# Pair 0 of an attention kernel: its split, its first scores and the last bias transfers in another place

## The chip, the cores and the metric

The kernel runs on one core of a Trainium2 chip. The metric is the device time of one execution in microseconds: 673.65 us is the median of three runs before the change (672.23 to 676.15). Times inside the trace count from the start of the span.

## The reference, cut to what matters

Attention with a bias that a small network computes from relative positions, then an MLP with ELU. There are 4 batches, 8 heads, 576 positions and 64 dimensions; the hidden size of the bias network is 32.

```python
scores = scale * np.matmul(q, k.transpose(0, 1, 3, 2))
x = (psi_rel / psi_i)[..., None]          # psi_rel = log1p|i-j|, psi_i = log1p(max(i,1))
h = np.maximum(x @ w1 + b1, 0.0)          # hidden 32
bias = h @ w2                             # one value per head
attn = softmax(scores + bias)             # over the last axis
x = (attn @ v) as (2304, 512)
out = elu(x @ w_in) @ w_out               # w_in 512 x 2048, w_out 2048 x 512
```

All arithmetic is float32 or better; the MLP's weights arrive as 64-bit floats and are decoded on the chip.

## The kernel before

The order of the instructions is written out by hand. Each engine takes its own in that order, and a waiting instruction holds up all that stand behind it on its engine. The program has three stages.

**The bias phase** (`bias_phase`, L130 to L257) makes the bias of all heads, in 36 sets of four position blocks each. A set takes four relus (L199 on ScalarE for g = 0, L201 on VectorE for the other three), eight matrix products into a pair of PSUM banks (`mix`, L209), and a scaled copy out of them (`place`, L222, ScalarE). Two sets make one buffer `bo`, and one transfer of 576 KB carries it into the tile `bias` (L231, on SyncE's queue); the sets of the small tile `biast` go in four transfers a buffer (L237). The relus run two sets ahead of the products. There are twelve relu buffers and four `bo` buffers. Sets 20 to 35 make the bias of the row chunks 2 and 3.

**Attention** (`attention`, L531 to L698) goes over 16 pairs of heads. For a pair, `load_pair` (five transfers, L98 to L102) fetches K and Q, and `split_high` and `split_low` (L118, L122) write each as a sum of a high and a low part; three products of those parts make the scores (`scores`, L299). Five chunks of rows are worked on, u = 0 to 4, u = 4 being the 64 last rows of both heads in one. For each, the order strings (L540) hold the steps: S the scores, X one head's step, which adds the bias and finds the row's extreme (L319, VectorE) and then takes the exponential (L330, ScalarE), T the transposes (L387), P the copies out of them (L406) into `pta` (chunks 0, 1, 4) or `ptb` (2, 3), V the product with the values, C the copy of the result, M and Q the 64 last columns. A token's letter `a` is the pair itself, `y` the pair before it, so a pair's later steps lie in the next pair's lines.

Before the change pair 0 follows the same five lines as the others: S0 X00 X01, S1 X10 X11, S4 T0 P00A X40, S2 T1 P01A P10A X20 X21, S3 T4 and so on. Its own split stands behind the last set (L255, L256; both halves on VectorE, while for later pairs the low half runs on GpSimd). Next come, on SyncE, the load of the first block of the MLP's weights (`decode`, L268), pair 0's values (L127) and, in line 2, pair 2's K and Q.

From pair 1 on, each pair also decodes a block of weights: `dm` from `raw` on VectorE (L277, in line 0, ahead of that pair's X00), `da` from `raw` on GpSimd (L273), the sign (L281), the shift (L283), the sum (L286).

Memory is handed out as a stack of pools. The pools of the bias phase (before the change `bc`, `bw` with the relus, `bop` with the `bo` buffers) are closed at its end, and the pools of the attention (`pta`, `ssp`, `ptb`, `xp`, `dq` with `da` and `dm`) take over the same bytes in order. PSUM has eight banks: four for score pairs (`sp`, also used by `mix`), three for transposes (`wp`), one for V (`vp`).

**The MLP** (L700 on) is a long run of matrix products.

Of the kernel before, what the change touches and what calls it, by code (L numbers as in the profile page):

```python
# [10 lines left out]
F32 = mybir.dt.float32  # L11
# [5 lines left out]
PSUM = bass.MemoryType.PSUM  # L17
# [7 lines left out]
def kernel(  # L25
# [11 lines left out]
    nc = tc.nc  # L37
# [21 lines left out]
    dpool = ctx.enter_context(tc.tile_pool(name="dpool", bufs=1, space=DRAM))  # L59
    ps1 = ExitStack()  # L60
    sp = ps1.enter_context(tc.tile_pool(name="sp", bufs=2, space=PSUM))
    wp = ps1.enter_context(tc.tile_pool(name="wp", bufs=3, space=PSUM))
    vp = ps1.enter_context(tc.tile_pool(name="vp", bufs=1, space=PSUM))
    ident = const.tile([P, P], F32, name="ident")

    bias = const.tile([P, NCH // 2, H, 2, S], F32, name="bias")
# [10 lines left out]
    qd = [[big.tile([P, P], F32R, name=f"qd{m}{i}") for i in range(2)] for m in range(2)]  # L77
    sts = [big.tile([P, S], F32, name=f"st{i}") for i in range(2)]

    def w_bank(name):  # L80
        return wp.tile([P, 512], F32, tag="w", name=name)

    def v_bank(name):
        return vp.tile([P, 512], F32, tag="v", name=name)

    def pair_bank(name):
        return sp.tile([P, 2, 512], F32, tag="ps", name=name)
# [41 lines left out]

    def bias_phase():  # L130
        with (
            tc.tile_pool(name="bc", bufs=1) as bc,
            tc.tile_pool(name="bw", bufs=12) as bw,
            tc.tile_pool(name="bop", bufs=4) as bop,
        ):


            NS = S // 16
            T = bc.tile([P, TW], F32, name="T")
            cs = bc.tile([P, 2 + 4 * H], F32, name="cs")  # L140
            psi = bw.tile([P, 4, NG], F32, tag="rel", name="psi")
            inr = bc.tile([P, 4, NS], F32, name="inr")
            SC = bc.tile([P, NS, 4], F32, name="SC")
            inv = bc.tile([P, NS // 4, 4], F32, name="inv")
            RIM = S - 64 + 48 + 3
            cut = RIM - P - 48


            def load_T(u0, u1, eng):
                for i in range(4):  # L150
                    row, off = (0, TOFF - RIM - 4 * i) if 4 * i <= TOFF - RIM else (i, TOFF + i - RIM - 4 * i)
                    hid = slice(32 * row, 32 * row + 32)
                    eng.dma_start(out=T[32 * i:32 * i + 32, u0:u1], in_=rtab[hid, u0 + off:u1 + off])

            tiny = bc.tile([P, 1], F32, name="tiny")
            for t in qd[0] + qd[1]:
                nc.gpsimd.memset(t.bitcast(F32), 0.0)
            nc.vector.memset(tiny, 0.0)
            for i in range(4):
                nc.scalar.dma_start(out=psi[32 * i:32 * i + 32], in_=cst[:, 0:NG].rearrange("(s c) n -> c s n", s=4))  # L160
            nc.sync.dma_start(out=cs, in_=cst[:, NG:NG + 2 + 4 * H])
            load_T(cut, RIM + S, nc.sync)
            load_T(0, cut, nc.sync)

            nc.scalar.activation(tiny, tiny, AF.Relu)
            for i in range(4):
                nc.scalar.dma_start(
                    out=inr[8 * i:8 * i + 8],
                    in_=cst[32 * i:32 * i + 32, NG + 2 + 4 * H:].rearrange("(s h) n -> h s n", s=4),
                )  # L170

            load_pair(0)
            load_pair(1)
            w1c, b1c = cs[:, 0:1], cs[:, 1:2]
            W2 = cs[:, 2:]

            for i in range(4):
                q = slice(32 * i, 32 * i + 32)
                sc = SC[q].rearrange("p k s -> p s k"), psi[q].rearrange("p s (k i) -> p s k i", i=4)[:, :, :, i]
                if i % 2:  # L180
                    nc.scalar.activation(*sc, AF.Copy, scale=b1c[q])
                else:
                    nc.vector.tensor_scalar(*sc, b1c[q], None, op0=ALU.mult)
            nc.vector.tensor_scalar(T[:, cut:RIM + S], T[:, cut:RIM + S], w1c, None, op0=ALU.mult)

            sets = [(2 * (c + o) + y, s) for c in (0, 2) for s in range(4) for y in range(2) for o in range(2)]
            sets[16:16] = [(2 * NCH, s) for s in range(4)]
            rels, pss = {}, {}

            def relu(s):  # L190
                B, x = sets[s]
                rels[s] = []
                for g in range(4):
                    u = RIM - 64 * B - 16 * g - x
                    src = T[:, u:u + S]
                    b = SC[:, 4 * B + g, x:x + 1]
                    rel = bw.tile([P, S], F32, tag="rel", name="rel")
                    if g == 0:
                        nc.scalar.activation(rel, src, AF.Relu, bias=b)  # L199
                    else:  # L200
                        nc.vector.tensor_scalar(rel, src, b, 0.0, op0=ALU.add, op1=ALU.max)  # L201
                    rels[s].append(rel)

            def mix(s):
                rel = rels.pop(s)
                ps = pss[s] = pair_bank("bps")
                for f in range(2):
                    for g in range(4):
                        nc.tensor.matmul(  # L209
                            ps[32 * g:32 * g + 32, f, 0:HS],  # L210
                            lhsT=W2,
                            rhs=rel[g][:, f * HS:(f + 1) * HS],
                            start=True,
                            stop=True,
                        )

            def place(s):
                if s % 2 == 0:
                    pss["bo"] = bop.tile([P, 2, S], F32, tag="bo", name="bo")
                bo = pss["bo"]  # L220
                B, x = sets[s]
                nc.scalar.activation(  # L222
                    bo[:, s % 2].rearrange("p (f x) -> p f x", f=2), pss.pop(s)[:, :, 0:HS],
                    AF.Copy, scale=inv[:, B, x:x + 1],
                )
                if s % 2 == 0:
                    return
                B, x = sets[s - 1]
                if B < 2 * NCH:
                    q0 = 64 * (B % 2) + x  # L230
                    nc.sync.dma_start(out=bias[q0:q0 + 61:4, B // 4], in_=bo)  # L231
                    return
                for e in range(2):
                    src = bo.rearrange("(i e) s x -> i e s x", e=2)[:, e]
                    for o in range(2):
                        q0 = TAIL * e + x + o
                        nc.sync.dma_start(out=biast[q0:q0 + 61:4], in_=src[:, o])  # L237

            AHEAD = 2
            for s in range(AHEAD):  # L240
                relu(s)
            for g in range(4):
                q = slice(32 * g, 32 * g + 32)
                nc.vector.tensor_copy(
                    inv[q].rearrange("p b s -> p s b"), inr[0:32].rearrange("p s (b g) -> p s b g", g=4)[:, :, :, g],
                )
            nc.vector.tensor_scalar(T[:, :cut], T[:, :cut], w1c, None, op0=ALU.mult)
            for s in range(NS):
                mix(s)
                if s > 0:  # L250
                    place(s - 1)
                if s + AHEAD < NS:
                    relu(s + AHEAD)
            place(NS - 1)
            split_high(0)  # L255
            split_low(0, nc.vector)  # L256
            decode(dp, 0, "load")  # L257

# [29 lines left out]
            nc.sync.dma_start(out=wf[f], in_=a.bitcast(F32))  # L288


    def scores(n, u):
        (kh, kl), (qh, ql) = nat[n]
        heads = range(2 if u < NCH else 1)
        st["ps", n, u] = [pair_bank("ps") for e in heads]
        for f in range(2):
            for t, (q, k) in enumerate(((0, kh), (0, kl), (1, kh))):
                for e, ps in zip(heads, st["ps", n, u]):
# [233 lines left out]
    def attention():  # L531

        pool = lambda name, bufs=1: ph1.enter_context(tc.tile_pool(name=name, bufs=bufs))
        pta, st["ssp"], ptb = pool("pta"), pool("ssp", 3), pool("ptb")
        xp = ph1.enter_context(tc.tile_pool(name="xp", bufs=2))
        st["dq"] = pool("dq")

# [8 lines left out]
        )  # L546
        LATE = (
# [45 lines left out]
        def step(N, line):  # L593
            for tok in line.split():
# [15 lines left out]
                if k == "S":  # L610
                    if i[0] == 0:
# [1 line left out]
                            pl.tile([P, NU, q], F32, tag=t, name=t)  # L613
                            for pl, t, q in ((pta, "pta", QA), (ptb, "ptb", QB))
                        ]
                    scores(n, i[0])
                elif k == "X":
                    expo(n, *i)
                elif k == "T":
# [26 lines left out]
        def aside(n, i):  # L646
            if i == 1:
                weights(n - 2, "store")
            if i == 0:
                load_v(n)  # L650
            if i == 2:
                if n + 2 < NP:
                    load_pair(n + 2)
            if n == 0 and i == 2:
                split_high(1)
                split_low(1)
            if n > 0 and n % HP == 0:
# [18 lines left out]
                high_w(1)  # L676

        for n in range(NP):
            for i, line in enumerate(STEPS if n < NP - 4 else LATE):
                flush()  # L680
                step(n, line)
                aside(n, i)
# [366 lines left out]
```

## Time and profile before

| | |
|---|---|
| median of three runs | 673.65 us (672.23 to 676.15) |
| the profiled execution | 670.85 us |
| its span | 668.7 us |
| TensorE busy | 651.7 us, 97% of the span |
| VectorE, ScalarE, GpSimd busy | 481.9, 450.1, 134.3 us |
| bias phase, products | 7.68 to 55.71 us |

A busy share is an average over all stages. Idle time of an engine costs only where something that ends the run waits for it, so the rows below are taken from single stretches. `PEld` is TensorE's weight load, `SPq` SyncE's queue, `ACTq`, `POOLq` and `DVEq` the sequencers of ScalarE, GpSimd and VectorE. A row such as `[0.62 <-issue]` says how long the engine had been idle and what ended that.

### The profile page before, as it was taken

Reading aid. Unit: us, or ns where it says so; the run is one execution under the profiler, and the core shown is the slowest. Engines: PE = TensorE matmul, PEld = TensorE weight load, DVE = VectorE, ACT = ScalarE, POOL = GpSimd, SP = SyncE. Lnnn points to the kernel's source line nnn. Section 1 sums busy time; section 2 is a strip of 40 time slices with the busy share of each in tenths; the row PEclk is TensorE's granted clock in tenths of the full one; section 3 lists DMA queues with packets and bytes.
Section 4 is the critical chain, followed back from the end, with each engine's and each line's share of the span. In section 5 each row is a group of like instructions: output and inputs, shape, how many; then the busy total and the mean of one; then the engine's idle time right before and its main releaser. Section 6 shows DMA issues by size and latency. Waiting matters only on the chain.

```text
span 668.7 us, 13838 instructions
## 1 busy us (share of the span) xinstructions
PE 651.7 (97%) x5246; PEld 522.8 (78%) x5246; DVE 481.9 (72%) x999; ACT 450.1 (67%) x981; POOL 134.3 (20%) x172
## 2 busy tenths in 40 slices
PE   5998999999999999999999999999999999999997
PEld 3545677777667677688898988989989898998986
DVE  6997888888888899887878998645465654444443
ACT  6996999999999899756655676544444544443343
POOL 0000655565566656410000000000000000000000
PEclk9997999999999999999999999999999999999999
DMA  6999557797677866664799669986854565454102
GB/s 161 217 228 243 160 176 196 227 268 225 197 234 222 261 194 173 214 208 124 238 326 348 250 265 341 351 302 223 264 196 196 203 255 238 196 197 174 64 1 94
DMA packets 49938, 144.63 MB, mean 216 GB/s; under 512 B 13376, under 2 KB 26448, under 8 KB 42192
## 3 DMA queue, kind: packets, MB, share of 16 engines
q1 hardware_dynamic: 47840, 141.08, 65.4%
q10 hardware_dynamic: 2032, 2.67, 1.2%
q8 instruction: 41, 0.67, 0.4%
q14 instruction: 25, 0.20, 0.1%
HBM read 92.14 MB, written 40.97 MB: 199 GB/s over the span
## 4 chain that ended last, share of the span: by engine, by line
PE 88%; DMA 4%; DVE 3%; ACT 2%; issue 1%; SPq 1%; POOL 0%; DVEq 0%; ACTq 0%; POOLq 0%
PE acc L793 29%; PE h L842 25%; PE wv L429 11%; PE ps L299 10%; PE bps L209 7%; PE wt L387 5%; DMA kk<-in_k_dram 1%; DMA raw<-in_wd_dram 1%; DVE ss L319 1%; PE wm L361 1%; DMA T<-in_rtab_dram 1%; DVE bias L518 1%; SPq L473 1%; DMA wa<-wf 1%; PE wt L395 0%
## 5 line engine op out<-in xcount | busy, mean ns | idle before, releaser
L793 PE MATMUL acc<-wB,gh 128*128 128x512 f32 x528 | 171.3, 392 | 0.0
L842 PE MATMUL h<-bias 128*128 128x384 f32 x552 | 111.6, 339 | 1.3 <-DVE e L821 1.3
L319 DVE CUSTOM_DVE_ANT_0 ss<-ps,bias 128x576 f32<-128x576 f32 x128 | 91.7, 753 | 24.4 <-PE ps L299 10.0
L793 PEld LDWEIGHTS acc<-wB,gh 128*128 128x128 f32 x528 | 98.1, 188 | 14.3
L842 PEld LDWEIGHTS h<-bias 128*128 128x128 f32 x552 | 99.7, 188 | 9.5 <-DVE e L821 2.4
L330 ACT ACTIVATE ss<-ss,nm 128x576 f32<-128x576 f32 x128 | 99.4, 780 | 10.0 <-DVE nm L319 9.6
L793 PE MATMUL acc<-wB,gl 128*128 128x512 f32 x264 | 103.8, 393 | 0.0
L822 ACT CAST gh<-e 128x384 fp32r<-128x384 f32 x96 | 49.4, 514 | 42.3 <-DVE e L821 41.4
L827 ACT ACTIVATE e<-c 128x384 f32<-128x384 f32 x66 | 34.7, 525 | 53.4 <-DVE c L873 53.4
L816 DVE TENSOR_TENSOR gl<-e,gh 128x384 fp32r<-128x384 f32 x96 | 53.1, 553 | 19.2 <-ACT gh L822 16.8
L827 ACT ACTIVATE e<-h 128x384 f32<-128x384 f32 x28 | 13.8, 491 | 68.3 <-PE h L842 68.3
L821 DVE SCALAR_TENSOR_TENSOR e<-e,c 128x384 f32<-128x384 f32 x66 | 36.7, 556 | 30.6 <-ACT e L828 30.5
L842 PE MATMUL h<-bias,wA 128*128 128x384 f32 x276 | 56.3, 338 | 0.0
L793 PEld LDWEIGHTS acc<-wB,gl 128*128 128x128 f32 x264 | 49.5, 187 | 7.8
L209 PE MATMUL bps<-rel,cs 128*32 128x288 f32 x576 | 48.0, 424 | 7.7 <-ACT rel L199 7.7
L429 PE MATMUL wv<-pta,vv 128*64 128x320 f32 (+1 forms) x320 | 53.6, 447 | 0.0
L842 PEld LDWEIGHTS h<-bias,wA 128*128 128x128 f32 x276 | 50.2, 188 | 3.8
L828 ACT ACTIVATE e<-e 128x384 f32<-128x384 f32 x96 | 50.5, 526 | 3.0
L299 PE MATMUL ps<-kh,qh 64*128 64x288 f32 x256 | 48.4, 345 | 3.1 <-DVE nm L319 2.6
L873 DVE TENSOR_TENSOR c<-h,u 128x384 f32<-128x384 f32 x66 | 36.7, 555 | 20.1 <-PE h L842 20.1
L387 PEld LDWEIGHTS wt<-ident,ss 64*128 64x128 f32 x1024 | 41.9, 140 | 9.6 <-issue 6.9
L333 POOL TENSOR_SCALAR md<-ss 128x128 f32<-128x128 f32 x64 | 22.2, 347 | 133.1 <-ACT ss L330 131.8
(127 smaller groups left out, 1195.7 us busy)
## 6 DMA issues: line engine op xcount, KB each, us to landing
wB<-wB SPq DMA_DIRECT2D x22, 1024.0 KB, 4.8
raw<-in_wd_dram SPq DMA_DIRECT2D x16, 1024.0 KB, 6.1
bias<-wA SPq DMA_DIRECT2D x9, 1792.0 KB, 9.0
wA<-wA SPq DMA_DIRECT2D x8, 1792.0 KB, 11.8
wa<-wf SPq DMA_DIRECT2D x20, 512.0 KB, 5.2
bias<-bo SPq DMA_DIRECT2D x16, 576.0 KB, 7.7
wA<-bias SPq DMA_DIRECT2D x5, 1792.0 KB, 14.4
wf<-da SPq DMA_DIRECT2D x16, 512.0 KB, 6.8
```

Source lines behind the costliest of these rows:

```text
L209: nc.tensor.matmul(ps[32 * g:32 * g + 32, f, 0:HS], lhsT=W2, rhs=rel[g][:, f * HS:(f + 1) * HS], start=True, stop=True,)
L299: nc.tensor.matmul(ps[:, f, 0:HS], lhsT=(qh, ql)[q][r, u * P:(u + 1) * P] if u < NCH else qd[n % 2][q], rhs=k[r, f * HS:(f + 1) * HS], sta ...
L319: nc.vector.tensor_tensor_reduce(out=s.rearrange("p (f x) -> p f x", f=2), in0=st["ps", n, u][e][:, :, 0:HS], in1=bap.rearrange("p (f x) - ...
L330: nc.scalar.activation(s, s, AF.Exp, bias=nm, scale=-1.0, accum_out=st["sm", b][:, hp, col:col + 1])
L387: nc.tensor.transpose(banks[r][:, x * TAIL:(x + 1) * TAIL], ss[q, c:c + P], ident[q, q])
L429: nc.tensor.matmul(st["pv", n, half][e * D:(e + 1) * D, 0:N], lhsT=l, rhs=r, start=start, stop=stop)
L793: nc.tensor.matmul(acc[j, t], lhsT=x[:, t * P:(t + 1) * P], rhs=w, start=(count[j, t] == 1), stop=(count[j, t] == 6 * NQ),)
L816: nc.vector.tensor_sub(gl, t, gh.bitcast(F32))
L822: nc.scalar.copy(g[i, e][0][:, h * HB:(h + 1) * HB], t)
L827: nc.scalar.activation(t, src, AF.Relu, scale=-1.0)
L828: nc.scalar.activation(t, t, AF.Exp, scale=-1.0)
L842: nc.tensor.matmul(ps, lhsT=a[f][c], rhs=x[y][c], start=(start and k == 0), stop=(stop and k == len(todo) - 1), skip_group_check=not start,)
```

## The change

Six things change.

1. PSUM: in the bias phase the four banks of `wp` and `vp` form a pool `ip` of two double banks; `open_banks` closes it behind line 1 of pair 0 and opens `wp` and `vp` there.
2. Pair 0's split moves from behind the last set to behind the relus that are issued with set 18.
3. Pair 0's S0 is issued ahead of set 31, into `ip`; its S1 goes into `ip` too.
4. Pair 0 gets an order of its own, FIRST: S4 stands ahead of X00, and each of the later scores earlier than in STEPS. Pair 1's split stands behind line 1.
5. Sets 33 and 35 send their buffer head by head, in eight transfers of 72 KB each. Heads 0 and 1 go at once; then come the weights, V of pair 0, heads 2 and 3 of both buffers, pair 2's K and Q, heads 4 to 7 of both.
6. The relu buffers become three pools of four, `psi` moves into a `bo` buffer, `bc` goes to the end of the stack, and `ssp` is opened ahead of `pta`.

```diff
+    ps0 = ExitStack()
+    ip = ps0.enter_context(tc.tile_pool(name="ip", bufs=2, space=PSUM))
+    def open_banks():
+        ps0.close()
+        for k, n in (("w", 3), ("v", 1)):
+            banks[k] = ps1.enter_context(tc.tile_pool(name=k + "p", bufs=n, space=PSUM))
...
-            tc.tile_pool(name="bw", bufs=12) as bw,
-            tc.tile_pool(name="bop", bufs=4) as bop,
+            tc.tile_pool(name="bw0", bufs=4) as bw0,
+            tc.tile_pool(name="bw1", bufs=4) as bw1,
+            tc.tile_pool(name="bw2", bufs=4) as bw2,
+            tc.tile_pool(name="bop", bufs=4) as bop,
             tc.tile_pool(name="bc", bufs=1) as bc,
...
-                    nc.sync.dma_start(out=bias[q0:q0 + 61:4, B // 4], in_=bo)
+                    dst = bias[q0:q0 + 61:4, B // 4]
+                    if s < NS - 4:
+                        nc.sync.dma_start(out=dst, in_=bo)
+                        return
+                    src = bo.rearrange("(k h) s x -> k h s x", h=H)
+                    parts = [(dst[:, h], src[:, h]) for h in range(H)]
+                    later.extend(parts[2:])
+                    send(parts[:2])
...
             for s in range(NS):
+                if s == NS - 5:
+                    scores(0, 0, first_bank)
                 mix(s)
...
+                if s == NS // 2:
+                    split_high(0)
+                    split_low(0, nc.vector)
             place(NS - 1)
-            split_high(0)
-            split_low(0, nc.vector)
             decode(dp, 0, "load")
+            load_v(0)
+            send(later[0:2] + later[6:8])
+            load_pair(2)
+            send(later[2:6] + later[8:])
...
-        pta, st["ssp"], ptb = pool("pta"), pool("ssp", 3), pool("ptb")
+        st["ssp"], pta, ptb = pool("ssp", 3), pool("pta"), pool("ptb")
+        FIRST = (
+            "aS0 aS4 aX00 aX01 aX40",
+            "aS1 aX10 aX11",
+            "aS2 aT0 aP00A",
+            "aT1 aP01A aP10A aX20 aX21",
+            "aS3 aT4 aP11V aP40A aP41A aX30 aX31",
+        )
-            if i == 0:
+            if i == 0 and n > 0:
                 load_v(n)
             if i == 2:
-                if n + 2 < NP:
+                if 0 < n < NP - 2:
                     load_pair(n + 2)
-            if n == 0 and i == 2:
+            if n == 0 and i == 1:
+                open_banks()
                 split_high(1)
                 split_low(1)
```

## Rows read from the trace of the kernel before

**Rows 1.** Stretches: length, busy time of each engine, granted clock, DMA share, GB/s.
```profile
80.00:90.00 10.00, 10.00 (x123) 6.84 (x122) 8.20 (x21) 9.45 (x26) 5.94 (x9) 1.00 0.41 103
58.50:65.30 6.80, 5.69 (x39) 4.77 (x41) 3.81 (x14) 3.62 (x9) 0.60 (x2) 0.50 1.01 245
64.50:68.50 4.00, 3.40 (x55) 3.05 (x52) 3.23 (x11) 3.57 (x8) 2.68 (x3) 0.90 1.02 320
```
**Rows 2.** Groups by line, 20 to 50 us: busy, mean ns, idle before.
```profile
L201 DVE TENSOR_SCALAR rel<-T,SC 128x576 f32<-128x576 f32 x71 | 30.6, 509 | 0.0
...
L209 PEld LDWEIGHTS bps<-rel,cs 128*32 128x32 f32 x370 | 14.3, 108 | 15.8 <-DVE rel L201 6.7 <-ACT bo L222 3.4
```
**Rows 3.** VectorE in order of time, end of the bias phase: start, length.
```profile
54.52 0.39 DVE L118 CAST qd<-qq 64x64 fp32r<-64x64 f32 x2
...
56.93 0.45 DVE L122 TENSOR_TENSOR qd<-qq,qd 64x64 fp32r<-64x64 f32 x2
58.00 0.76 DVE L319 CUSTOM_DVE_ANT_0 ss<-ps,bias 128x576 f32<-128x576 f32 x1 [0.62 <-issue]
```
**Rows 4.** The chain of waits, 55 to 78 us: start, length, what.
```profile
55.74 0.75 ACT bo L222
...
59.50 1.58 PE ps L299 x10
...
73.81 0.98 PE ps L299 x9
...
76.35 0.79 PE ps L299 x6
```
**Rows 5.** ScalarE in order of time, pair 0.
```profile
58.80 0.78 ACT L330 ACTIVATE ss<-ss,nm 128x576 f32<-128x576 f32 x1 [2.32 <-DVE nm L319]
...
59.58 0.76 ACT L330 ACTIVATE ss<-ss,nm 128x576 f32<-128x576 f32 x1
...
66.19 1.06 ACT L406 COPY pta<-wt 128x512 f32<-128x512 f32 x2
...
70.59 0.76 ACT L330 ACTIVATE ss<-ss,nm 128x576 f32<-128x576 f32 x1
```
**Rows 6.** VectorE in order of time, pairs 0 and 1.
```profile
65.98 0.76 DVE L319 CUSTOM_DVE_ANT_0 ss<-ps,bias 128x576 f32<-128x576 f32 x1 [0.25 <-PE ps L299]
...
69.25 0.75 DVE L319 CUSTOM_DVE_ANT_0 ss<-ps,bias 128x576 f32<-128x576 f32 x1
...
69.92 0.69 DVE L277 TENSOR_SCALAR dm<-raw 128x1024 int32<-128x1024 uint32 x1
71.34 0.76 DVE L319 CUSTOM_DVE_ANT_0 ss<-ps,bias 128x576 f32<-128x576 f32 x1 [0.72 <-PE ps L372]
...
74.84 0.76 DVE L319 CUSTOM_DVE_ANT_0 ss<-ps,bias 128x576 f32<-128x576 f32 x1
```
**Rows 7.** SyncE's issues in order of time.
```profile
57.09 0.58 SPq L268 DMA_DIRECT2D raw<-in_wd_dram  x1
57.73 1.82 SPq L127 DMA_DIRECT2D vv<-in_v_dram  x1
59.65 0.52 SPq L98 DMA_DIRECT2D kk<-in_k_dram  x1
...
61.54 1.32 SPq L102 DMA_DIRECT2D qq<-in_q_dram  x2
```
**Rows 8.** Issues in ns and landings in us: of `biast`, of `kk`, of `bias`.
```profile
L237 SPq DMA_DIRECT2D biast<-bo x8: 533/561/595, 32.1 to 38.1; - x8
...
DMA to landing us min/median/max: 2.3/2.5/2.7
...
DMA to landing us min/median/max: 7.2/7.7/8.5
```
**Rows 9.** Semaphore rows ahead of the first write of `da` and of `ptb`.
```profile
L273 POOLq EVENT_SEMAPHORE  x4: 17/43/43, 71.5 to 71.7; - x4
...
L406 ACTq EVENT_SEMAPHORE  x2: 38/38/38, 72.1 to 72.2; - x2
```

More of the change, by code (lines that the diff above doesn't have):

```diff
@@ L61 @@
     sp = ps1.enter_context(tc.tile_pool(name="sp", bufs=2, space=PSUM))
-    wp = ps1.enter_context(tc.tile_pool(name="wp", bufs=3, space=PSUM))
-    vp = ps1.enter_context(tc.tile_pool(name="vp", bufs=1, space=PSUM))
+    ps0 = ExitStack()
+    ip = ps0.enter_context(tc.tile_pool(name="ip", bufs=2, space=PSUM))
+    banks = {}
     ident = const.tile([P, P], F32, name="ident")
@@ L78, with first_bank @@
     sts = [big.tile([P, S], F32, name=f"st{i}") for i in range(2)]
+    def open_banks():
+        ps0.close()
+        for k, n in (("w", 3), ("v", 1)):
+            banks[k] = ps1.enter_context(tc.tile_pool(name=k + "p", bufs=n, space=PSUM))
     def w_bank(name):
-        return wp.tile([P, 512], F32, tag="w", name=name)
+        return banks["w"].tile([P, 512], F32, tag="w", name=name)
     def v_bank(name):
-        return vp.tile([P, 512], F32, tag="v", name=name)
+        return banks["v"].tile([P, 512], F32, tag="v", name=name)
+    def first_bank(name):
+        return ip.tile([P, 2, 512], F32, tag="ps", name=name)
     def pair_bank(name):
@@ L140, in bias_phase @@
             cs = bc.tile([P, 2 + 4 * H], F32, name="cs")
-            psi = bw.tile([P, 4, NG], F32, tag="rel", name="psi")
+            psi = bop.tile([P, 2, S], F32, tag="bo", name="psi")[:, 0].rearrange("p (s n) -> p s n", s=4)
             inr = bc.tile([P, 4, NS], F32, name="inr")
@@ L196, in relu @@
                     b = SC[:, 4 * B + g, x:x + 1]
-                    rel = bw.tile([P, S], F32, tag="rel", name="rel")
+                    rel = (bw0, bw1, bw2)[s % 3].tile([P, S], F32, tag="rel", name="rel")
                     if g == 0:
@@ L237, in place, with send @@
                         nc.sync.dma_start(out=biast[q0:q0 + 61:4], in_=src[:, o])
+            later = []
+            def send(parts):
+                for dst, src in parts:
+                    nc.sync.dma_start(out=dst, in_=src)
             AHEAD = 2
@@ L288, in decode, with scores @@
             nc.sync.dma_start(out=wf[f], in_=a.bitcast(F32))
-    def scores(n, u):
+    def scores(n, u, bank=pair_bank):
         (kh, kl), (qh, ql) = nat[n]
         heads = range(2 if u < NCH else 1)
-        st["ps", n, u] = [pair_bank("ps") for e in heads]
+        st["ps", n, u] = [bank("ps") for e in heads]
         for f in range(2):
@@ L615, in step @@
                         ]
-                    scores(n, i[0])
+                    if ("ps", n, i[0]) not in st:
+                        scores(n, i[0], first_bank if (n, i[0]) == (0, 1) else pair_bank)
                 elif k == "X":
@@ L678, in attention @@
         for n in range(NP):
-            for i, line in enumerate(STEPS if n < NP - 4 else LATE):
+            for i, line in enumerate(FIRST if n == 0 else STEPS if n < NP - 4 else LATE):
                 flush()
```

## The prediction

> **What bounds the kernel now.** I began with the table by stretches. From about 70 us on TensorE is full (10.00 of 10 us in [rows 1], first row) and VectorE is not (8.20), and the page keeps it so to the end; a microsecond that pair 0 or the bias phase gives or takes is therefore given or taken by the whole span. Then the groups by line in the bias phase: VectorE's three relus of a set stand with no idle time (71 in 30.6 us, 0.0 idle, [rows 2]), while TensorE's weight loads idle 15.8 us of the same 30, mostly for those relus. 30.6/71 is 0.43 us a relu, 1.29 us a set: VectorE sets the pace of the bias phase. Third, VectorE's own rows at the end of it [rows 3]: the last relu is followed by pair 0's split, 54.52 to 57.38, and then VectorE waits for TensorE, 0.62 us before the first score-plus-bias step (X00). The chain of waits [rows 4] runs from ScalarE's last copy over pair 0's scores (1.58 us for what takes 0.98 at 73.81) into a run of TensorE alone, and the granted clock is 0.50 from 58.5 to 65.3 us ([rows 1], second row). Last come ScalarE [rows 5], VectorE in pair 1 [rows 6] and SyncE's issues [rows 7].
>
> I write S, X, T, V as in the order strings, and X00(1) for pair 1.
>
> **Part 1, the split amid the sets.** The same eight instructions, 57.38 - 54.52 = 2.86 us [rows 3], move into a queue that has no gap [rows 2]. Nothing on VectorE hides them, so every later relu, the last matrix products and ScalarE's last scaled copy come 2.86 us later: that copy, 55.74 to 56.49 [rows 4], ends at 59.35. In the old place about 1.9 us of them lay beside TensorE's and ScalarE's last set. TensorE starves some 2 us at set 21. Below: no further cost, the value I take, since it waits half its time anyway [rows 2]. Above: the clock falls to the lower level as at 58.5 [rows 1] and two sets take 0.6 us longer, +1.3 us (an estimate: a set's 1.29 us less the idle half, doubled).
>
> **Part 2, scores ahead.** Pair 0's S0 now sits ahead of set 31 on TensorE, in banks of its own: about 0.9 us beside waits for relus, cost 0 (0 to 0.5). VectorE goes from its last relu (57.4) straight into X00 at 57.4 and X01 at 58.1 instead of 58.00 and 58.69 [rows 3]. TensorE leaves set 35 at about 58.4; S4 takes 1.0 (its tail is 0.79 at the higher clock, [rows 4]) and S1 0.9 more, so X40 starts at 59.5, X10 at 60.3, X11 ends at 61.8, pair 1's three casts take 1.1, and X20 follows at 62.9. S3 needs the banks of X20 and X21; X31 starts at 66.1, against 69.25 [rows 6]: 3.1 us earlier. ScalarE is behind that: the first exp waits for the scaled copy, 59.3 (58.80 before). To the last exp of the pair lie eight pitches of 59.58 - 58.80 = 0.78, three copies of 0.53 and two smaller ones (0.4 each, an estimate from the 0.53), 8.6 in all [rows 5]: 67.9 against 70.59, 2.7 earlier. So this part, with part 1 inside it, would give **-2.7 us**, if nothing after it waited. The first two pieces of the last set's bias are issued at 59.4 and 60.0 and land by 62.5, so X20 hardly waits (before it waited 0.25 for TensorE, [rows 6]).
>
> **Part 3, the transfers by head.** Here is what is late next. Two issues of 576 KB become 16 of 72 KB, four of them ahead of the weight load. After the last scaled copy SyncE now has 21 issues in one run. Their pace: pieces of the small bias tile cost 0.56 us each and 0.04 between [rows 8], so 0.6; weight load to V load 0.64, V load to the next 1.92, pair 2's five issues 59.65 to 62.90, 3.25 [rows 7]. The last of the 21 starts at 59.4 + 2 x 0.6 + 0.64 + 1.92 + 4 x 0.6 + 3.25 + 7 x 0.6 = 73.0, and lands 2.5 later by the K rows [rows 8]: 75.5. With the 533 ns minimum for every piece, 0.6 for the V load and 2.3 of landing it is 73.1; with half the issue time for an eighth of the rows, 70.1; a second slow issue makes 77.4. I take **74.5**, near the sum by the nearest rows.
>
> Who waits for that? The late pieces read the `bo` buffers, whose memory the attention's pools take over. The trace shows how such a takeover is guarded: the first write of `ptb` carries two extra semaphore rows and the first write of `da` four, with up to two semaphores each [rows 9]. By the sizes in the code `ptb` covers only the start of the first `bo` buffer before the change, so I read the guard as one over the whole pool. After the change `ptb`, `xs`, `da` and the first 768 bytes of `dm` lie over `bo` (bw0 to bw2 take 27,648 bytes, `bo` up to 46,080, `dm` starts at 45,312). The first write of `dm` is L277 on VectorE, at 69.92 before [rows 6], free to go at 66.9 now, and it would wait until 74.5. Queued behind it: X00(1), X01(1), the sign and shift steps, X10(1). P30A on ScalarE and the scale on GpSimd wait for the same pieces, and neither ends later than VectorE's chain. Before, nothing of this showed, because the last bias transfer, issued behind 56.49, had landed by 65 (8.5 us at most, [rows 8]).
>
> Price: X10(1) comes 0.69 + (74.84 - 71.34) after the wait (L277's own time and the way from X00(1) to X10(1), [rows 6]), so 78.7 against 74.84, +3.8. TensorE's S4(1) uses up about 0.5 of that (its tail stands at 76.35, X10's bank is free at 75.6): **+3.3** in place of -2.7. In the meantime TensorE finishes pair 0's products near 71 and idles until X01(1) ends at 76.6, 5 us, and after far shorter pauses the clock fell before ([rows 3], then [rows 1], second row). S1(1) stood at 73.81 and the full queue follows it [rows 4]. At half speed what follows loses 0 (all of it covered by VectorE's chain) to 2.5 us (5 us of the 6.8 that the lower level lasted, uncovered); I take **+0.9**, for the 1.8 us between S1(1) and S4(1).
>
> **Sum**: -2.7 replaced by +3.3, plus 0.9: +4.2 us. The profiled execution took 670.85 us (span 668.7 and 2.15 around it), so 675.05; the median of the three runs shown is 673.65, 2.8 above it, and on that scale the forecast is **677.9 us**.
>
> [...]
>
> **Rivals.**
> A, the other side: the guard does not reach `dm` and its fellows (the pieces' reads are tracked buffer by buffer, or the pool lies elsewhere). Then part 2's -2.7 stands from the first exp on: 671.0. For it: L277 started directly behind X31 before the change [rows 6]. Against: [rows 9], and VectorE had by then passed X20, which needs the same transfers.
> B, the pieces are bound by bytes and not by issues. After 59.4 the queue carries about 2.97 MB; at 320 GB/s ([rows 1], third row) that is 9.3 us, and with 2.3 of landing 71.0. L277 then waits 4 us, X10(1) is at 75.2 and S4(1) about on time: +0, 673.7. It decides for "no change" below 72. Against: eight issues cannot start faster than [rows 7, 8] show.
> C, X20 of pair 0 itself waits for all pieces, because all write the same tile. X20 goes from 65.98 to 74.5: +8.5, 682.2. Against: X00 started at 58.00 before, while the last transfer to the same tile, issued behind 56.49, needed at least 7.2 us [rows 8].
>
> **Numbers.** Forecast 0.64, A 0.17, B 0.12, C 0.07. About 0.5%, 3.4 us, is what a measurement of this kernel can tell from no change: 670.3 to 677.0 is "same". The forecast's own spread (70.1 to 77.4 for the landing, 0 to 2.5 and 0 to 1.3 for the clock) is 672 to 681, two thirds of it above 677.0; with C, slower 0.49. A reaches below 670.3 in a third of its cases: faster 0.06; same 0.45. The range takes in A's centre and leaves out half of C's: 670.9 to 681.5.
>
> **What would show it.** Part 1: the last scaled copy starts near 58.6, and the relus have a 2.9 us hole with L118 and L122 in it. Part 2: X00 directly behind the last relu, X31 near 66.1, the pair's last exp near 67.9. Part 3: SyncE's last bias piece starts between 70 and 73.5, and L277 starts only after it has landed, with VectorE idle for 6 to 8 us before it and a DMA as the releaser. If L277 starts near 67, the forecast is wrong and A holds; if VectorE idles before X20, C does.

## The result and the profile after

The changed kernel takes 681.43 us (median of six, 678.5 to 684.2) against 673.65: ratio 1.0110, 95% interval [1.0076, 1.0145], some 7.5 us slower (5 to 10 by the interval). Ratios, here and below, are of the means of the executions, those more than 1.5% above the fastest of their kernel left out, and so differ a little from the ratios of the medians. The profiled execution is the slowest of the six: 684.2 us, span 682.4 (before 670.85 and 668.7). I take positions from it up to 90 us only. Of its 13.35 us, 7.7 are there by pair 1; a further 4.6 come at 232 us in a wait for a weight load, told at the end.

The table by stretches of the changed kernel (length, busy time of each engine, granted clock, DMA share, GB/s):
```profile
60.00:70.00 10.00, 7.75 (x104) 6.87 (x106) 6.78 (x19) 9.33 (x26) 4.18 (x8) 0.83 0.71 217
70.00:80.00 10.00, 3.60 (x29) 2.38 (x31) 3.57 (x7) 2.31 (x7) 1.85 (x2) 0.72 0.40 116
80.00:90.00 10.00, 10.00 (x112) 7.26 (x111) 6.09 (x18) 7.35 (x19) 6.00 (x7) 0.77 0.57 180
```
The second row is the damage: between 70 and 80 us every engine is idle for more than half the time, and DMA is busy 0.40 of it. So it isn't bandwidth that is missing: [rows 1] have 320 GB/s, this row 116.

VectorE of the changed kernel in order of time (start, length, line, what, and in brackets the idle time before it and what ended it):
```profile
35.13 0.39 DVE L127 CAST qd<-qq 64x64 fp32r<-64x64 f32 x2
...
37.54 0.45 DVE L131 TENSOR_TENSOR qd<-qq,qd 64x64 fp32r<-64x64 f32 x2
...
57.84 0.76 DVE L350 CUSTOM_DVE_ANT_0 ss<-ps,bias 128x576 f32<-128x576 f32 x1 [0.41 <-ACT bo L233]
...
63.48 0.74 DVE L350 CUSTOM_DVE_ANT_0 ss<-ps,bias 128x576 f32<-128x576 f32 x1
...
67.46 0.75 DVE L350 CUSTOM_DVE_ANT_0 ss<-ps,bias 128x576 f32<-128x576 f32 x1
...
76.43 0.69 DVE L308 TENSOR_SCALAR dm<-raw 128x1024 int32<-128x1024 uint32 x1 [8.21 <-DMA bias<-bo]
77.04 0.75 DVE L350 CUSTOM_DVE_ANT_0 ss<-ps,bias 128x576 f32<-128x576 f32 x1
...
80.52 0.76 DVE L350 CUSTOM_DVE_ANT_0 ss<-ps,bias 128x576 f32<-128x576 f32 x1 [0.30 <-PE ps L330]
...
84.87 0.76 DVE L350 CUSTOM_DVE_ANT_0 st<-ps,biast 128x576 f32<-128x576 f32 x1 [0.96 <-PE ps L330]
```
In order: the split amid the relus, X00, X20 (no wait), X31, then the first write of `dm` (L277 before, L308 now) behind 8.21 us of nothing, X00 of pair 1, X10(1) and X40(1). X31 is 1.8 us ahead of [rows 6]; X10(1) is 5.7 us behind it. X40(1) of the kernel before is this row:
```profile
77.18 0.76 DVE L319 CUSTOM_DVE_ANT_0 st<-ps,biast 128x576 f32<-128x576 f32 x1 [0.37 <-PE ps L299]
```
X40(1) is thus 7.7 us later, and that stays (8.0 at pair 11): TensorE is full from there on (137.90 of 138 us from 90 to 228 us), so X40(1) is a good mark for the whole span. I use it below.

The first write of `dm` carries what `da` and `ptb` carried before [rows 9], four semaphore rows (operation, count, ns, first and last start):
```profile
L308 DVEq EVENT_SEMAPHORE  x4: 21/50/50, 74.5 to 76.3; - x4
```
SyncE's issues of the changed kernel, answering to [rows 7]:
```profile
57.77 3.16 SPq L261 DMA_DIRECT2D bias<-bo  x4
60.98 0.93 SPq L299 DMA_DIRECT2D raw<-in_wd_dram  x1
61.96 0.43 SPq L136 DMA_DIRECT2D vv<-in_v_dram  x1
62.43 2.47 SPq L261 DMA_DIRECT2D bias<-bo  x4
...
68.42 1.39 SPq L111 DMA_DIRECT2D qq<-in_q_dram  x2
69.86 5.01 SPq L261 DMA_DIRECT2D bias<-bo  x8
```
In that run SyncE waited 0.7 us for the weight load to land (at L109) and 1.0 us for the V load (at L111).

The chain of waits, answering to [rows 4]:
```profile
61.96 6.38 DMA vv<-in_v_dram
...
74.28 2.02 DMA bias<-bo
...
78.53 2.05 PE ps L330 x12
...
83.45 1.38 PE ps L330 x6
```
The chain enters DMA twice. SyncE stands from about 67.4 until the V load has landed (68.34) before it issues a Q load; later the last piece, issued at 74.28, lands at 76.30 and lets VectorE go. Behind it S1(1) takes 2.05 us for 0.98 and S4(1) 1.38 for 0.79, at the lower clock (granted 0.50 from 74.4 to 84.6 us, 1.00 from 84.6 to 90; TensorE had last worked until about 72.1). From the start of S1(1) to the end of S4(1) TensorE works without a break, and X40(1) follows directly: 6.30 us (78.53 to 84.83), where the kernel before takes 3.33 (73.81 to 77.14, [rows 4]). So the 7.7 us of X40(1) are 4.7 of a later start of S1(1) and 3.0 of a longer stretch.

### The profile page after: what moved, and what is told of

The parts are those of the page before. It is cut to its first block, busy times and chain, and to the rows that moved or that the text cites. A ratio compares the mean times of both kernels' runs of the same rounds, so it can differ in the third digit from the quotient of the medians.

```text
span 682.4 us, 13840 instructions
## 1 busy us (share of the span) xinstructions
PE 652.7 (96%) x5246; PEld 522.6 (77%) x5246; DVE 481.7 (71%) x999; ACT 450.4 (66%) x981; POOL 134.8 (20%) x172
## 4 chain that ended last, share of the span: by engine, by line
PE 83%; DMA 5%; DVE 4%; ACT 2%; issue 2%; POOL 1%; SPq 1%; POOLq 0%; DVEq 0%; ACTq 0%
PE acc L833 28%; PE h L882 25%; PE wv L460 11%; PE ps L330 10%; PE wt L418 5%; PE bps L220 3%; DVE rel L212 2%; DMA raw<-in_wd_dram 1%; DMA vv<-in_v_dram 1%; PE wm L392 1%; SPq L261 1%; DMA wa<-wf 1%; DMA T<-in_rtab_dram 1%; POOL xr L526 1%; PE wt L426 0%
## 5 line engine op out<-in xcount | busy, mean ns | idle before, releaser
L330 PEld LDWEIGHTS ps<-kh,qh 64*128 64x128 f32 x256 | 27.4, 191 | 30.0 <-DVE nm L350 22.0
```

Of the source, the lines that this page charges most:

```text
L330: nc.tensor.matmul(ps[:, f, 0:HS], lhsT=(qh, ql)[q][r, u * P:(u + 1) * P] if u < NCH else qd[n % 2][q], rhs=k[r, f * HS:(f + 1) * HS], sta ...
```

## Experiments

Theory: the takeover of the deferred pieces' memory costs the time, as Part 3 said. Main rival (R1): the split, the new order or the run of 21 issues cost it directly. Each experiment has its own runs of the kernel before on its chip, and ratios are against those.

**e1: the deferred pieces' buffers moved away from the first `dm`.**
```
-  tc.tile_pool(name="bop", bufs=4) as bop,
+  tc.tile_pool(name="bop", bufs=2) as bop,   # then bc, a gap, and
+  tc.tile_pool(name="bol", bufs=2) as bol,   # under the second da and dm
-  pss["bo"] = bop.tile(...)
+  pss["bo"] = (bol if s // 2 % 4 < 2 else bop).tile(...)
-  ... tag="da", bufs=2 ...  tag="dm", bufs=2
+  ... tag=f"da{f % 2}" ...  tag=f"dm{f % 2}"    # order in dq: da0 dm0 da1 dm1
```


> The changed kernel with one thing moved in memory: the buffers that the deferred pieces read (those of sets 33 and 35) lie in a pool of their own, over which only the second da and the second dm tile come to lie, so that the first write of dm, ptb, xs and the first da has no deferred piece to wait for. Order, issues and split are those of the changed kernel. Theory (the guard over the old pool is what makes the change slower): L308 starts directly behind X31 at about 68.2 us instead of 75.7, with no DMA as its releaser; S4 of pair 1 ends about 10 us earlier, X40 of pair 1 goes from +7.7 to about -2 against the kernel before, and the time is 671 to 672 us, 0.3 to 0.4% under the kernel before and 1.4% under the changed one. Rival R1 (the split amid the sets, the new order of pair 0 or the 21 issues in one run cost the time themselves): 679 to 682 us, as the changed kernel. Rival R2 (half and half: the late pieces hold up the loads of pair 2 and V as well): about 676 us.

Measured 681.31 us, ratio 1.0101 [1.0046, 1.0155]: my number failed, R1's held. But the rows said something else than R1 (the semaphores of the line, then VectorE; L311 is the old L308):
```profile
L311 DVEq EVENT_SEMAPHORE  x4: 21/50/50, 75.1 to 76.9; - x4
```
```profile
77.03 0.69 DVE L311 TENSOR_SCALAR dm<-raw 128x1024 int32<-128x1024 uint32 x1 [9.49 <-DMA bias<-bo]
```
The wait is still there, and so are the four semaphore rows, although by its address the first `dm` touches none of the pieces' buffers. `ptb`, which lies in a pool of its own, had lost three of its four semaphore rows. What is left in common is the *pool*: `dq` holds all four tiles and as a whole reaches over `bol`, the pool of the pieces' buffers.

**e5: same addresses, two pools.**
```
-  st["dq"] = pool("dq")
+  st["dq0"], st["dq1"] = pool("dq0"), pool("dq1")   # da0 dm0 | da1 dm1
```


> The kernel of e1_clear (buffers of the deferred pieces in a pool of their own, at the same addresses), with the da and dm tiles shared out over two pools instead of one: the first da and dm lie in a pool that touches none of the deferred pieces' buffers, the second da and dm in a pool that lies over them exactly. No address changes against e1_clear. Theory as revised (a pool's first tiles wait for every old tile that the pool as a whole touches, not for what the tile itself covers): L308 loses its four semaphore rows and starts directly behind X31, near 68; X00 of pair 1 near 70, X10 near 73.5 to 74.5; X40 of pair 1 stands -2 to 0 us against the kernel before and the time is 670.5 to 673 us. Rival (the first write of dm waits for the order of the transfers themselves, say for a queue that must be drained before memory of the bias phase is used again): no change against e1_clear, 681 us. Rival R1 (split and order cost the time as well): 674 to 677 us.

VectorE of e5 (first `dm`, then X00, X10 and X40 of pair 1):
```profile
67.78 0.69 DVE L311 TENSOR_SCALAR dm<-raw 128x1024 int32<-128x1024 uint32 x1
69.08 0.76 DVE L353 CUSTOM_DVE_ANT_0 ss<-ps,bias 128x576 f32<-128x576 f32 x1 [0.60 <-PE ps L406]
...
72.97 0.76 DVE L353 CUSTOM_DVE_ANT_0 ss<-ps,bias 128x576 f32<-128x576 f32 x1
...
75.31 0.76 DVE L353 CUSTOM_DVE_ANT_0 st<-ps,biast 128x576 f32<-128x576 f32 x1 [0.36 <-PE ps L333]
```
671.48 us, ratio 0.9969 [0.9942, 0.9996]. No DMA in front of L311, X40(1) 1.9 us ahead of the kernel before. Nothing but the grouping of four tiles differs from e1, no order, no address, no transfer; the V load that SyncE issues behind the last piece even goes later than in the changed kernel (76.2 for 74.92). So the takeover is guarded pool against pool, and without its wait the change isn't slow: (1.0110 - 0.9969) x 673 = 9.5 us. This version also beats the kernel before, by 0.3%, with an interval that ends just short of 1.

**e4: only `dm` clear of the old pool.**
```
+  gap = pool("gap").tile([P, 192], F32)
+  st["dqm"] = pool("dqm")
-  dec["m", f] = st["dq"].tile(...)
+  dec["m", f] = st["dqm"].tile(...)
```


> The changed kernel with 768 bytes of padding in memory below dm, so that dm alone clears the old pool of the deferred pieces; da, xs and ptb still lie over it. Theory: VectorE's L308 starts behind X31, near 68.2, with no DMA as its releaser, and X00 and X01 of pair 1 follow near 69 to 70; but the first write of ptb (P30A, on ScalarE) and the scale on GpSimd still wait for the last piece at 76.3, and with them the first da; the shift and X10 of pair 1 come near 78 instead of 80.5. X40 of pair 1 goes from +7.7 to +4 to +6, the time to 677 to 680 us. Rival R5 (only the wait of dm matters, the others are covered): X40 of pair 1 near -2 and 671 to 672 us. Rival R1 (split and order cost the time): 681 us.

VectorE, GpSimd and ScalarE of e4:
```profile
68.06 0.69 DVE L308 TENSOR_SCALAR dm<-raw 128x1024 int32<-128x1024 uint32 x1
...
78.95 0.69 DVE L314 TENSOR_SCALAR da<-da 128x1024 uint32<-128x1024 uint32 x1 [6.10 <-DMA vv<-in_v_dram]
```
```profile
77.78 1.14 POOL L304 TENSOR_SCALAR da<-raw 128x1024 f32<-128x1024 f32 x1 [7.53 <-DMA bias<-bo]
```
```profile
77.71 0.58 ACT L437 COPY ptb<-wt 128x512 f32<-128x512 f32 x1 [5.63 <-DMA bias<-bo]
```
679.27 us, 1.0078 [1.0040, 1.0115], X40(1) +5.2. `dm` goes free, and the scale on GpSimd and P30A on ScalarE take its place: VectorE waits again, one step further on, in the shift (the releaser named there, a V load, had nothing to do with it; it stands behind GpSimd's scale). A guard that holds three engines must be lifted for all three. By the addresses of the built program the first `da` touches neither buffer of the pieces, and the last piece reads a buffer that ends just below `dq`: the old pool, too, is guarded as a whole.

**e9: the landing moved, the guard left.**
```
-  send(later[0:2] + later[6:8]); load_pair(2); send(later[2:6] + later[8:])
+  send(later); load_pair(2)
```


> The changed kernel with the order of the deferred issues changed alone: all twelve pieces directly behind the V load, the five K and Q loads of pair 2 behind them. Memory and everything else as in the changed kernel. Theory (the price is the time at which the last piece lands, one for one, and that time is made of issues in a row and of the wait of SyncE for the V load's landing): the last piece starts near 71 instead of 74.2 and lands near 73.5 (72 if nothing holds SyncE for the V load); L308 starts then instead of at 76.4, X40 of pair 1 stands +3.3 to +4.9 us against the kernel before instead of +7.7, the time is 676.5 to 679 us. Rival (bytes, not issues, set the landing): it lands near 76 all the same and the time stays at 681. Rival (the K and Q loads of pair 2 now come late for its split): X20 of pair 1 waits for a DMA and part of the gain is lost again.

SyncE and VectorE of e9:
```profile
63.21 0.45 SPq L136 DMA_DIRECT2D vv<-in_v_dram  x1
63.70 9.24 SPq L261 DMA_DIRECT2D bias<-bo  x12
```
```profile
74.55 0.69 DVE L307 TENSOR_SCALAR dm<-raw 128x1024 int32<-128x1024 uint32 x1 [6.80 <-DMA bias<-bo]
```
678.85 us, 1.0059 [1.0023, 1.0095]; X40(1) +5.1, just over the range I gave, because the landing (74.4) was 0.9 later than said (the profiled execution, 684.27 us, is the slowest of the twelve). L307 starts 1.9 us earlier than in the changed kernel and X40(1) stands 2.5 earlier; the other 0.6 is TensorE's stretch from S1(1) to S4(1), 5.64 us here for 6.30. The landing's time is the price, and the order of issues sets it, not their bytes. Pair 2's loads, now behind, hold up nothing here: X20(1) waits for TensorE, 0.28 us, and not for a DMA.

**e2: part 3 undone, parts 1 and 2 kept.** Sets 33 and 35 go as one transfer each:
```
-  if s < NS - 4: ...                      # below it the eight parts, six of them deferred:
-  later.extend(parts[2:]); send(parts[:2])
+  nc.sync.dma_start(out=dst, in_=bo)
```


> The changed kernel with the transfers by head undone: sets 33 and 35 go as one transfer of 576 KB each, behind their last copies, as in the kernel before; split, order and the moved loads stay. Theory: two issues instead of sixteen, so the last bias transfer is issued near 59.8 us and lands near 66 to 68; X20 may wait for it up to 4 us, L308 no more than 1 us; X40 of pair 1 stands -2 to +2 us against the kernel before and the time is 672 to 676 us. Rival R1 (split and order cost the time): 679 to 682 us. Rival R3 (the bytes bound the landing, not the issues): the last byte lands near 74 to 76 all the same, X20 itself waits for it, and the time is above 684 us.

VectorE of e2 (X20, then `dm`, then X10(1)):
```profile
66.38 0.76 DVE L344 CUSTOM_DVE_ANT_0 ss<-ps,bias 128x576 f32<-128x576 f32 x1 [2.79 <-issue]
...
70.96 0.69 DVE L302 TENSOR_SCALAR dm<-raw 128x1024 int32<-128x1024 uint32 x1
...
78.23 0.76 DVE L344 CUSTOM_DVE_ANT_0 ss<-ps,bias 128x576 f32<-128x576 f32 x1 [1.88 <-PE ps L324]
```
676.38 us, 1.0042 [1.0008, 1.0077], X40(1) +3.4, a little more than said: X20 waited 2.79 us (the row names no releaser; in the chain its semaphore rows start at 66.15, 6.3 us after the last bias transfer was issued, at 59.83), and the granted clock of 70 to 80 us was 0.65. Neither rival's time came. So the pieces do what they are for, X20 is 2.9 us earlier with them; the guard then took more than that back.

**e8: part 1 alone**, the kernel before with the split moved amid the sets.
```
-  split_high(0); split_low(0, nc.vector)      # behind the last relu
+  if s == NS // 2: split_high(0); split_low(0, nc.vector)
```


> The kernel before with part 1 alone: pair 0's split amid the sets instead of behind the last relu. Theory (VectorE has no gap amid the sets, the 2.86 us go whole into the bias phase, and about half of them were covered in the old place): the last scaled copy 2.3 to 2.9 us later, X00 of pair 0 at 59.5 instead of 58.0, and from there on everything 1 to 2 us later: 674 to 675 us against 672.9. Rival (the transfers set the pace and the split lies beside them): X00 near 57, 1 us less than before, 671.5 to 672 us.

VectorE of e8, X00 of pair 0:
```profile
61.32 0.76 DVE L320 CUSTOM_DVE_ANT_0 ss<-ps,bias 128x576 f32<-128x576 f32 x1 [3.12 <-PE ps L300]
```
676.79 us, 1.0040 [1.0010, 1.0070]. The split costs more than I had said: X00 is 3.3 us later than [rows 3], not 1.5. S0 needs banks that ScalarE's last scaled copy empties, and that copy starts at 59.45, 3.7 us later than in [rows 4]: the 2.86 us stood on the path in full, and where the other 0.9 come from stays open. With part 2 that S0 is out of the way, and from e8 to e5 the time falls by (1.0040 - 0.9969) x 673 = 4.8 us.

**e6: the split's subtractions on GpSimd, in e5.**
```
-  split_low(0, nc.vector)
+  split_low(0)                                  # GpSimd
```


> e5_two_pools, and the four subtractions of pair 0's split (1.76 of its 2.86 us) on GpSimd instead of VectorE, in the same place amid the sets. Theory (VectorE sets the pace of the bias phase, so what it is spared there comes back whole): the bias phase ends 1.7 us earlier than in e5_two_pools and the time is 1 to 1.8 us less, 669 to 671.5 us. Rival (GpSimd's reads slow the relus that run beside it, or the bias phase's transfers set the end): no change, or up to 1 us more than e5_two_pools.

GpSimd, then VectorE of e6:
```profile
36.27 17.93 POOL L131 TENSOR_TENSOR kl<-kk,kh 128x576 fp32r<-128x576 f32 x1 [34.37 <-DMA bias<-bo]
54.16 1.26 POOL L131 TENSOR_TENSOR ql<-qq,qh 128x512 fp32r<-128x512 f32 x1
```
```profile
36.10 16.83 DVE L215 TENSOR_SCALAR rel<-T,SC 128x576 f32<-128x576 f32 x39
58.91 1.38 DVE L215 TENSOR_SCALAR rel<-T,SC 128x576 f32<-128x576 f32 x3 [5.97 <-PE bps L223]
```
677.07 us, 1.0057 [1.0034, 1.0080]: 5.9 us slower than e5. One subtraction, 1.42 us elsewhere in the same trace, took 17.93. It began with a run of 39 relus without a gap (36.10 to 52.93) and ended at 54.20, 1.27 us after the last of them, about its usual length. S0 of pair 0, amid the sets, waited for it, and the sets behind S0 with it. In the 16.83 us of unbroken relus GpSimd finished nothing; by what it was held up no run shows.

**e10: three relus of VectorE on ScalarE, in e5.**
```
-  if g == 0:
+  if g == 0 or g == 1 and s in (21, 22, 23):
       nc.scalar.activation(rel, src, AF.Relu, bias=b)
```


> e5_two_pools, and three of VectorE's relus (the second of the sets 21, 22 and 23) on ScalarE, which has nothing to do while VectorE works on pair 0's split. Theory (the 2.86 us of the split stand in full on the path of the bias phase, and ScalarE idles beside them): three relus of 0.43 us off VectorE, the bias phase ends 1.0 to 1.3 us earlier, the last scaled copy near 58.2 instead of 59.3; 670 to 670.5 us, 1 us less than e5_two_pools, which is about what two such medians can tell. Rival (ScalarE, with 0.77 us for each, is the pace itself): no change, or the copies later by up to 0.6 us.

The chain of waits of e10:
```profile
58.09 0.74 ACT bo L236
...
69.19 3.12 PE wv L463 x12
```
673.38 us, 0.9994 [0.9962, 1.0026]: no gain that can be measured. The bias phase did end 1.2 us earlier (the last copy at 58.09 against 59.31 in e5), as said; but the pair's products then fell into the lower clock (granted 0.92 from 60 to 70 us and 0.90 from 70 to 80, against 1.00 in e5), 3.12 us where e5 takes 1.76 for twelve, and X40(1) stands at -1.5, not ahead of e5's -1.9. One profile each; whether the clock takes such a gain back every time stays open.

**e3, e7, e11: dummy products ahead of S1(1)**, to see what the lower clock costs. The changed kernel and, ahead of S1(1),
```
+  for k in range(40):   # e3, into pair 1's own banks; e7: 36, e11: 48, into a bank wx = w_bank("wx")
+      nc.tensor.matmul(..., lhsT=nat[0][0][0][:, 0:P], rhs=nat[0][0][0][:, 0:128], start=True, stop=True)
```


> The changed kernel with 40 dummy matrix products of 128 columns on TensorE just ahead of pair 1's S1, into columns of its banks that nothing reads, in the time in which TensorE otherwise idles for the first dm. They add work that the result doesn't need. Theory (of the 7.8 us, some 2 to 2.5 come from the lower clock after the wait and the rest from the wait): the granted clock of 74 to 84 us rises from the lower level for part of it, S1 of pair 1 takes about 1 us instead of 2.05, X40 of pair 1 goes from +7.7 to about +5.5 and the time to about 679 us; if the dummy products all end well before the wait does, the clock falls all the same and nothing changes (681.4). Rival R4 (the clock is covered by VectorE's chain and costs nothing): no change, 681.4 us, although the clock is up.

> The changed kernel with 36 dummy matrix products of 128 columns on TensorE ahead of pair 1's S1, into a bank of the transposes that nothing waits for (in e3_warm they wrote pair 1's score banks and stood behind X00 and X01). They fill TensorE's idle time from 73.3 to 78.5 us; their result is not used. Theory (some 2 to 2.5 of the 7.8 us are the lower clock after the wait): the granted clock stays up or returns sooner, S1 of pair 1 takes 1.0 to 1.6 us instead of 2.05 and the time is 678.5 to 680 us. Rival (the clock is covered): 681 us with the clock up. Rival (the products run at the lower clock, 0.22 us each as in e3_warm, and end after 79 us): 681 to 684 us.

> e7_warm_free with 48 dummy products instead of 36 (0.118 us each there, 4.24 us from 73.16, with 3.4 us of idle time left behind them and S1 of pair 1 still at the lower clock). They would end near 78.8. Theory (the lower clock costs 1 to 2 of the 7.8 us): with less than 2 us left idle the granted clock stays at the upper level, S1 of pair 1 takes 1.0 us instead of 2.05 and X40 of pair 1 follows L308 by 7.3 us as in e1_clear instead of 8.4; 679 to 680.5 us. Rival (covered by VectorE's chain): L308 to X40 stays at 8.4 us with the clock up, 681 us.

TensorE of e3, then TensorE and VectorE of e11:
```profile
78.95 8.79 PE L656 MATMUL ps<-kh 128*128 128x128 f32 x40 [5.64 <-ACT pta L407]
```
```profile
73.46 5.60 PE L657 MATMUL wx<-kh 128*128 128x128 f32 x48
80.11 0.98 PE L330 MATMUL ps<-kh,qh 64*128 64x288 f32 x2 [1.05 <-DVE nm L350]
```
```profile
85.35 0.76 DVE L350 CUSTOM_DVE_ANT_0 st<-ps,biast 128x576 f32<-128x576 f32 x1 [0.36 <-PE ps L330]
```
e3 failed as a test: its products wrote the banks that X00(1) and X01(1) still had to read, so they stood behind the wait and not in it. It shows what a microsecond of TensorE is worth there: 8.79 us of products, X40(1) 8.4 us later than in the changed kernel (688.39 us, 1.0213 [1.0162, 1.0265]). From `dm` to X40(1) it is 7.3 us in e11 (78.01 to 85.35), 8.0 in e7, 8.4 in the changed kernel, and 7.3 in e1, which has no dummy products at all. The chain of e1, for its stretch from S1(1) to S4(1):
```profile
79.13 2.05 PE ps L333 x12
...
83.50 0.79 PE ps L333 x6
```
S1(1) ran at the lower clock in all four (2.05 us in the changed kernel and e1; in e7 and e11 its later pairs of products take 0.68 us each, 0.67 in the changed kernel and 0.29 in the kernel before); what differs is when the upper level came back. By the mean granted clock of 80 to 90 us (0.77, 0.71, 0.83 and 0.86 in the changed kernel, e7, e11 and e1) that was near 84.6, 85.8, 83.7 and 82.8, an estimate that takes 0.50 until then and 1.00 after (in e11 0.50 from 80.4 on, which fits 0.72 from 78 to 84 us and 0.60 from 79.6 to 83.4); S1(1) starts at 78.53, 80.81, 80.11 and 79.13. The stretch takes 6.30 us in the changed kernel, 5.82 in e7, 5.20 in e11, 5.16 in e1. So the 1.1 us between 8.4 and 7.3 are not the price of the lower clock but of a later return, and as e1 has the same return without dummy products, nothing shows that these helped. In e11 they took 0.117 us each (0.22 in e3, where the granted clock of 80 to 90 us was 0.50), TensorE then idled 1.05 us, and from 79.6 to 83.4 us the granted clock was 0.60. Less than 2 us of idle time did not keep the clock up there, against what I had expected. No run here has the upper level through S1(1) behind such a wait. An estimate of the whole price from rows: in the changed kernel X10(1) would have started at 80.22 without its 0.30 us of waiting for TensorE; from X10(1) to X40(1) it is 2.34 us in the kernel before and in e5 at the upper clock (1.00 from 70 to 80 us in both); X40(1) would have stood near 82.6 instead of 84.87, some 2.3 us earlier. In the times none of this shows: e7 679.17 us (1.0091 [1.0056, 1.0126]), e11 683.05 (1.0123 [1.0077, 1.0170]), the changed kernel 1.0110. The landing hides it: it came at 76.3, 76.9, 77.6, 78.6 and 77.9 us in the profiled executions of the changed kernel, e1, e4, e7 and e11, with one order of issues (in e7 and e11 by the start of the first `dm`, 78.71 and 78.01, which follows the landing by 0.13 us in the changed kernel). Inconclusive in the time.

## Why the prediction was right, and where its size was off

The direction and the mechanism were right; the size was not: +4.2 us forecast, some 7.5 to 7.8 measured, 677.9 against 681.43. That the time lies inside the stated range, 0.07 us below its upper end, is luck: the end had been drawn for part of rival C, which fell, and the forecast's own spread ended at 681. Two terms were too small, the landing and the clock. Term by term:

- **Part 1.** The split stands where it was put (2.86 us, 35.13 to 37.99) and the last scaled copy starts at 59.04 instead of 58.6, 0.4 later. TensorE's starving at set 21 didn't lower the clock (1.00 from 30 to 40 us in the runs shown). Right but for the 0.4; e8 shows the cost uncovered. (One reading in the prediction was loose: of the weight loads' 15.8 us of idle time [rows 2] names VectorE's relus for 6.7, not for most. VectorE's pace stands in its own row and doesn't hang on it.)
- **Part 2.** X00 57.84 (said 57.4), X20 63.48 without a wait (62.9), X31 67.46 (66.1), the last exp at 69.00 against 70.59, 1.6 earlier, not 2.7. Part of that is a lower clock that the sum didn't have: 0.50 from 64.2 to 67.5 us in the profiled execution, with X31 9.6 us behind X00, against 1.00 and 8.9 us in e1. The gain without the guard, -2.7 in the text, came out in e5 as -1.9 at X40(1) and (1 - 0.9969) x 673 = -2.1 in the time. A little too large.
- **Part 3, the landing.** This is the term that was mis-sized: 74.5 in the text, 76.3 measured. The sum by the nearest rows had given 75.5, and I took 1.0 off it for possibilities that no row showed. Against that 75.5 the rows stand as follows: the start 0.4 later (59.81 instead of 59.4), the pieces 0.4 longer in all, weight load to V load 0.98 instead of 0.64, V load to the next 0.47 instead of 1.92, pair 2's five issues 4.86 instead of 3.25, the last landing 2.02 instead of 2.5; together +0.8. The five issues hold waits that I hadn't seen: the eighth issue behind the weight load and the eighth behind the V load (66.92 and 68.42) both start late, 0.7 and 1.0 us, and the view of SyncE's waits names those two loads; the second goes just as the V load has landed. In e9, with pieces standing where the K and Q loads stood, the chain again waits for the V load, which lands at 69.59, and goes on with the eighth issue behind it at 69.61. So in these runs an issue waited for a transfer eight issues back.
- **Part 3, the wait.** The first `dm` (8.21 us) and GpSimd's scale (6.25) waited, as said; P30A stands behind the exponential of X00(1) in the changed kernel, and its own wait shows only in e4 (5.63). The reason I gave, a guard over the whole *old* pool, was half of it: e1 and e5 show that the new pool counts as a whole too. By addresses alone e1 should have been fast.
- **The clock.** X10(1) to X40(1) was to cost 0.4 (0.9 of clock, 0.5 of slack used up); it cost 2.0 (from +5.7 to +7.7). These 1.6 us and the landing's (X10(1) at +5.7 instead of +3.8, 1.9) make up the 3.5 us between 4.2 and 7.7. The term that was too small is the clock: I charged half speed for the 1.8 us between S1(1) and S4(1), 0.9 us, but the whole stretch from S1(1) to the end of S4(1) ran at the lower level (0.50 to 84.6 us), 6.30 us for 3.33, 3.0 more, of which the estimate above leaves some 2.3 uncovered. No run has the wait without the lower clock, so how the 2.0 would split between clock and slack isn't measured. The far shorter pauses of the text are TensorE's 0.41 us before 56.54 and 0.95 before 58.82 in the kernel before.
- **Rivals.** A failed, but its price was good: without the guard 671.0 was forecast and e5 takes 671.48. B (bytes set the landing) fell with e9, and with 116 GB/s in the idle stretch. What the pieces cost is their issue: 0.59 us for each, beside 2.02 from the last issue to its landing, and the issues stand in a row on SyncE. C fell: X20 has no wait in the changed kernel.

## What to carry to other kernels

A transfer that is put off for its consumer's sake also puts off the day on which its *source* memory is free; look for what will lie there next, and at the pool it belongs to, not only at the tile. When a wait seems to come from memory, split or regroup pools at equal addresses (e5) before believing that the order is to blame: between e1 and e5 the grouping of four tiles was worth (1.0101 - 0.9969) x 673 = 8.9 us. And where many small transfers replace few, add up the issues in a row (0.59 us each here), with what each of them waits for, before adding up bytes.

## What the runs showed of the hardware

- While VectorE ran 39 relus without a gap, one GpSimd subtraction beside them took 17.93 us instead of 1.42 (e6).
- In e11 TensorE worked until 79.06 (48 dummy products of 0.117 us), idled 1.05 us, and from 79.6 to 83.4 us the granted clock was 0.60.
- In the changed kernel two issues on SyncE waited for the landing of the transfer eight issues before them, 0.7 and 1.0 us; in e9 the eighth issue behind the V load started at 69.61, as that load landed (69.59).
- In the profiled runs of one order of issues the last landing varied by 2.3 us (76.3 to 78.6): now and then the issue of a piece took 1.3 to 1.9 us instead of 0.6 (1.62 in e1, 1.37 and 1.31 in e4, 1.93 in e9).
- VectorE waits once, between 218 and 233 us, for the weight load that `dm` reads, and by very different times: 0.87 us in the kernel before, 1.26 in e11, 1.55 in e2, 4.06 in e9, 4.22 in the changed kernel and 4.92 in e5, one profiled execution each; e11 and the changed kernel differ by dummy products only. The kernel before, the changed kernel and e5:
```profile
221.27 0.69 DVE L277 TENSOR_SCALAR dm<-raw 128x1024 int32<-128x1024 uint32 x1 [0.87 <-DMA raw<-in_wd_dram]
```
```profile
232.64 0.69 DVE L308 TENSOR_SCALAR dm<-raw 128x1024 int32<-128x1024 uint32 x1 [4.22 <-DMA raw<-in_wd_dram]
```
```profile
223.47 0.69 DVE L311 TENSOR_SCALAR dm<-raw 128x1024 int32<-128x1024 uint32 x1 [4.92 <-DMA raw<-in_wd_dram]
```
In e5, which is faster than both, it costs the most; a single execution of e5 (674.98 us here, 669.08 at best) says little by itself. That is why X40(1) and medians, not spans, carry the argument above.
